# Attention with cached K and V on one core: another order of the first loads and of the first projections

## Chip, cores and metric

One Trainium2 chip, one NeuronCore. The metric is the device time of one execution in microseconds (us), lower is better. The core has TensorE (matmuls; PE in the profile, its weight loads PEld), VectorE (DVE), ScalarE (ACT), GpSimd (POOL) and SyncE (SP); loads are issued by SP and by ScalarE, each on a queue of its own.

## The reference

Two independent problems A and B of the same shape; in each, 16 batches of 80 rows, 32 query heads on 16 K/V heads of 512 cached keys, head size 128:

```
q = (x @ wq) as [batch, 32 heads, 80, 128]          x: [16, 80, 576], wq: [576, 4096], bf16
scores = q @ k^T * 128**-0.5                        k, v: [16, 16, 512, 128], two query heads per K/V head
o = softmax(scores) @ v
out = o as [16, 80, 4096] @ wo                      wo: [4096, 576]
result = concat(A's out, B's out, axis=-1)          [16, 80, 1152]
```

## The kernel before

The work is cut into 128 units: a unit U is one batch and four K/V heads, so 8 query heads of 80 rows. Eight batches (a half) follow each other with the same four K/V heads. Units 0 to 7 are the first half of A's batches, units 8 to 15 the second half, with the same quarter of wq.

For each half and quarter (`goct`) q is projected: operation `qp goct.i.c` (L672) multiplies five chunks of x, transposed, with the 128 columns of head i, for the batches of part c. For the very first one (`goct` 0) part 0 is batches 0 and 1 (160 columns) and part 1 is batches 2 to 7 (480 columns); later ones take four and four (320 columns). VectorE or ScalarE moves the result to `qT` (`qev`, L683 and L684). A's x is loaded by rows (`ldx`, L547) in row blocks of 128, transposed on TensorE (`xtr`, L562) and moved to `xT` (`xev`, L566).

A unit has 640 score rows of 512 keys: five tiles of 128 rows. The first tile gathers the remainders of the four heads (`qkr`, L782: four 32-column matmuls side by side), the others are `qk` (L796). Remainder tiles of two units are done together, except that units 0 and 1 stand alone; so the score groups are unit 0, unit 1, units 2 and 3, units 4 and 5, and so on. Each tile then goes through the maximum on VectorE (`max`, L805), exp with row sums on ScalarE (`exp`, L809), the reciprocal (`rcp`, L815), a scaling on GpSimd (`nrm`, L818), four transposes on TensorE (`tr`, L824) and a copy to `pT` on VectorE (`ptev`, L830 and L832). `pv` (L870) multiplies with V; `oev` (L886) moves the result to `oT`; the output projection is L923. K comes by a transposing load on SP (`ldk`, L746), V by a plain one (`ldv`, L750), the first four V on SP and later ones on ScalarE's queue.

The order on each engine is not written out: a planner (`_Sched`) takes operations with keys, durations and streams and places them greedily, with a model of the two load queues (`_Dma`), and the resulting order is fixed at build time. On the chip each engine runs its list in order and waits on semaphores. Operations of one stream on one engine keep the order of their keys. `XLD` and `WQ1` hold the keys of the first loads of x and wq. Before the first useful matmul TensorE runs `warm` (L507), eight matmuls on ones, and between the transposes of x blocks 1 and 2 `warm2` (L522), four more.

The first loads before, in order, on SP: x of the first half in two pieces (2 and 3 row blocks), x of the second half in two pieces, K of unit 0, the second 1024 columns of wq in four pieces, K of units 1, 2, 3, V of units 0, 1, K of unit 4, V of units 2, 3, K of unit 5. On ScalarE: the first 1024 columns of wq in four pieces.

TensorE's order before: `xtr` of blocks 0 and 1, `warm2`, `xtr` of blocks 2 to 4, then `qp` of heads 0 to 3 for batches 0 and 1, of heads 0 to 3 for batches 2 to 7, of heads 4 to 7 for batches 0 and 1, of head 4 for batches 2 to 7, and then the first score group, with the rest of the projections among the scores.

## Time and profile before

| what | us |
|---|---|
| median of 3 runs | 772.09 (771.92 to 772.26) |
| the profiled execution: its own time | 772.67 |
| the profiled execution: span of its instructions | 770.9 |
| TensorE busy | 762.3 |
| VectorE, ScalarE, GpSimd busy | 680.0, 607.2, 432.3 |

The profile is of one execution; its times start at its first instruction. A row of the timeline gives start, length, engine, line, operation, output and input, shape and count; a row of an engine with a q (SPq, ACTq) is the issuing of a load, not the load itself. The landing of a load is its issue plus the time to landing in the profile's DMA view. Matmuls are pipelined: a single one is listed with some 0.2 to 0.4 us, and in a stream they start every 56 ns (128 columns), 69 (160), 136 (320), 203 (480) or 216 (512).

### The profile page before, as it was taken

Reading aid. Unit: us, or ns where it says so; the run is one execution under the profiler, and the core shown is the slowest. Engines: PE = TensorE matmul, PEld = TensorE weight load, DVE = VectorE, ACT = ScalarE, POOL = GpSimd, SP = SyncE. Lnnn points to the kernel's source line nnn. Section 1 sums busy time; section 2 is a strip of 40 time slices with the busy share of each in tenths; the row PEclk is TensorE's granted clock in tenths of the full one; section 3 lists DMA queues with packets and bytes.
Section 4 is the critical chain, followed back from the end, with each engine's and each line's share of the span. In section 5 each row is a group of like instructions: output and inputs, shape, how many; then the busy total and the mean of one; then the engine's idle time right before and its main releaser. Section 6 shows DMA issues by size and latency. Waiting matters only on the chain.

```text
span 770.9 us, 21081 instructions
## 1 busy us (share of the span) xinstructions
PE 762.3 (99%) x7942; PEld 575.7 (75%) x7942; DVE 680.0 (88%) x1599; ACT 607.2 (79%) x1695; POOL 432.3 (56%) x647
## 2 busy tenths in 40 slices
PE   9899999999999999999999999999999999999998
PEld 5577777777777777777777777777777777777786
DVE  4999999899899999999989989988888988899972
ACT  1888987888888888877778877878888888888860
POOL 1556655655656565655555645654656655565650
PEclk9999999999999999999999999999999999999999
DMA  9999999999999999999999999999999999999931
GB/s 245 235 235 244 217 262 217 228 213 228 206 208 226 248 258 255 239 233 228 205 219 202 220 258 238 249 238 241 220 194 207 198 207 240 241 243 241 248 96 31
DMA packets 422660, 170.76 MB, mean 222 GB/s; under 512 B 319264, under 2 KB 422176, under 8 KB 422560
## 3 DMA queue, kind: packets, MB, share of 16 engines
q1 hardware_dynamic: 355872, 103.22, 74.4%
q10 hardware_dynamic: 66688, 66.20, 29.9%
q8 instruction: 64, 1.05, 0.6%
q14 instruction: 36, 0.29, 0.1%
HBM read 87.46 MB, written 2.95 MB: 117 GB/s over the span
## 4 chain that ended last, share of the span: by engine, by line
PE 94%; DVE 4%; DMA 1%; ACT 1%; issue 0%; SPq 0%
PE ps L672 22%; PE ps L923 20%; PE ps L870 18%; PE ps L824 16%; PE ps L796 13%; PE ps L782 4%; DVE negmax L805 2%; DVE pT L832 1%; DMA acc<-in_A_x_dram 1%; ACT p_sb L809 0%; DVE qT L684 0%; DVE xT L566 0%; DVE pT L830 0%; ACT oT L886 0%; PE ps L562 0%
## 5 line engine op out<-in xcount | busy, mean ns | idle before, releaser
L818 POOL TENSOR_SCALAR p_sb<-p_sb,rinv 128x512 bf16<-128x512 bf16 x640 | 429.9, 692 | 315.6 <-DVE rinv L815 315.4
L809 ACT ACTIVATE p_sb<-ps,negmax 128x512 bf16<-128x512 f32 x640 | 438.8, 691 | 63.8 <-DVE negmax L805 53.9
L805 DVE TENSOR_REDUCE negmax<-ps 128x1 f32<-128x512 f32 x640 | 427.5, 682 | 17.8 <-PE ps L782 9.6
L832 DVE COPY pT<-ps 128x512 bf16<-128x512 bf16 x512 | 210.2, 417 | 15.8 <-PE ps L824 13.3
L870 PE MATMUL ps<-pT,v_sb 128*128 128x160 bf16 x2048 | 219.1, 233 | 0.3 <-issue 0.2
L824 PE MATMUL ps<-ident,p_sb 128*128 128x128 bf16 x2248 | 214.6, 219 | 0.3 <-DVE pT L832 0.2
L672 PE MATMUL ps<-xT,wq_sb 128*128 128x320 bf16 (+2 forms) x1280 | 212.6, 299 | 0.8 <-ACT p_sb L809 0.6
L870 PEld LDWEIGHTS ps<-pT,v_sb 128*128 128x128 bf16 x2048 | 163.3, 98 | 42.5 <-issue 2.0
L796 PE MATMUL ps<-kT,qT 128*128 128x512 bf16 x512 | 193.0, 379 | 1.0 <-ACT p_sb L809 1.0
L824 PEld LDWEIGHTS ps<-ident,p_sb 128*128 128x128 bf16 x2248 | 159.8, 98 | 37.4 <-DVE pT L832 5.9
L923 PE MATMUL ps<-wo_sb,oT 128*128 128x288 bf16 x1280 | 171.3, 286 | 0.1
L672 PEld LDWEIGHTS ps<-xT,wq_sb 128*128 128x128 bf16 x1280 | 116.7, 98 | 54.0 <-ACT oT L886 3.8
L923 PEld LDWEIGHTS ps<-wo_sb,oT 128*128 128x128 bf16 x1280 | 122.7, 98 | 34.2 <-issue 2.1
L886 ACT CAST oT<-ps 128x320 bf16<-128x320 f32 x256 | 108.6, 424 | 44.7 <-PE ps L870 42.0
L809 ACT ACTIVATION_READ_ACCUMULATOR p_sb<-ps,negmax 128x1 f32 x640 | 130.3, 204 | 0.0
L684 DVE TENSOR_SCALAR qT<-ps 128x320 bf16<-128x320 f32 (+2 forms) x138 | 67.4, 488 | 13.4 <-PE ps L672 12.1
L683 ACT ACTIVATE qT<-ps 128x320 bf16<-128x320 f32 (+1 forms) x118 | 51.1, 433 | 31.4 <-PE ps L672 30.9
L796 PEld LDWEIGHTS ps<-kT,qT 128*128 128x128 bf16 x512 | 50.0, 98 | 5.6 <-ACT p_sb L809 2.4
L951 DVE TENSOR_TENSOR osb<-ps,acc 128x288 bf16<-128x288 f32 x40 | 18.3, 457 | 26.9 <-PE ps L923 26.5
L782 PE MATMUL ps<-kT,qT 128*32 128x512 bf16 x512 | 39.6, 384 | 1.9 <-ACT p_sb L809 1.9
L815 DVE RECIPROCAL rinv<-rowsum 128x1 f32<-128x1 f32 (+2 forms) x206 | 34.3, 168 | 6.0 <-ACT p_sb L809 5.7
L830 DVE COPY pT<-ps 128x512 bf16<-128x512 bf16 x50 | 20.8, 416 | 2.3 <-PE ps L824 2.0
(19 smaller groups left out, 47.0 us busy)
## 6 DMA issues: line engine op xcount, KB each, us to landing
v_sb<-in_B_v_cache_dram ACTq DMA_DIRECT2D x64, 512.0 KB, 4.8
v_sb<-in_A_v_cache_dram ACTq DMA_DIRECT2D x60, 512.0 KB, 5.1
wo_sb<-in_A_wo_dram SPq DMA_DIRECT2D x16, 288.0 KB, 5.5
wo_sb<-in_B_wo_dram SPq DMA_DIRECT2D x16, 288.0 KB, 5.0
wq_sb<-in_B_wq_dram SPq DMA_DIRECT2D x16, 256.0 KB, 4.8
out_dram<-osb SPq DMA_DIRECT2D x40, 72.0 KB, 3.3
v_sb<-in_A_v_cache_dram SPq DMA_DIRECT2D x4, 512.0 KB, 5.0
wq_sb<-in_A_wq_dram SPq DMA_DIRECT2D x8, 256.0 KB, 5.1
```

Source lines behind the costliest of these rows:

```text
L672: last = e.matmul(ps[:, vb.phys, 0:n1 - n0], lhsT=wq_sb[:, wsl, ck, i * 128:(i + 1) * 128], rhs=xT[:, half, ck, n0:n1], start=(ck == 0), s ...
L684: return e.tensor_scalar(dst, src, SCALE, None, op0=AluOpType.mult)
L782: last = e.matmul(ps[32 * g4:32 * g4 + 32, vb_.phys, :], lhsT=qT[:, qp_, g4 * 160 + 128:g4 * 160 + 160], rhs=kT[:, ks_, :, g4 * 128:(g4 + ...
L796: return e.matmul(ps[:, vb.phys, :], lhsT=qT[:, qp, gl * 160:gl * 160 + 128], rhs=kT[:, ks, :, gl * 128:(gl + 1) * 128], start=True, stop= ...
L805: return e.tensor_reduce(negmax[:, si:si + 1], ps[:, vb.phys, :], axis=AX.X, op=AluOpType.max, negate=True)
L809: return e.activation(p_sb[:, psl, :], ps[:, vb.phys, :], AF.Exp, bias=negmax[:, si:si + 1], scale=1.0, accum_out=rowsum[:, ss, k:k + 1])
L818: return e.tensor_scalar(p_sb[:, psl, :], p_sb[:, psl, :], rinv[:, ss, k:k + 1], 1.0, op0=AluOpType.mult, op1=AluOpType.mult)
L824: last = e.transpose(psb[:, vt.phys, j * 128:(j + 1) * 128], p_sb[:, psl, j * 128:(j + 1) * 128], ident[:])
L832: return e.tensor_copy(pT[:, pts, :, 0:4, gl * 32:gl * 32 + 32], psb[:, vt.phys, 0:512].rearrange("p (j h c) -> p j h c", j=4, h=4))
L870: last = e.matmul(ps[:, vo.phys, off:off + 160], lhsT=v_sb[:, vs, gl, j * 128:(j + 1) * 128], rhs=pT[:, pts, j, :, gl * 32:gl * 32 + 32], ...
L886: return e.copy(dst, src)
L923: last = e.matmul(ps[:, vb.phys, 0:DC], lhsT=oT[:, hi, rb * 128:(rb + 1) * 128], rhs=wo_sb[:, hi, c3 * DC:(c3 + 1) * DC], start=(hi == 0), ...
```

## The change

The first loads get another order and are cut differently:

- x of the first half comes in three pieces: block 0 on SP, block 1 on ScalarE's queue, blocks 2 to 4 on SP.
- The first 512 columns of wq come in three pieces: chunks 0 and 1 on SP behind the first x piece; chunk 4, and chunks 2 and 3, on ScalarE's queue. The next 512 columns follow on SP.
- Then on SP: K of unit 0, columns 1024 to 1535 of wq, K of unit 1, columns 1536 to 2047, K of units 2 and 3, V of unit 0, x of the second half in two pieces, V of unit 1, K of units 4 and 5, V of units 2 and 3.
- Each of these wq pieces has a semaphore of its own, and so has each of the five pieces of later wq loads per buffer.
- The transposed block 1 of x is moved to `xT` by ScalarE, not VectorE.
- `warm` has seven matmuls; `warm2` and the memset behind it are gone.
- On TensorE `qp` of heads 0 and 1 for batches 0 and 1 comes before the transposes of blocks 2 to 4, then those of heads 2 to 7 for batches 0 and 1, then heads 0 and 1 for batches 2 to 7, then the first score group; the other six for batches 2 to 7 lie among the scores of units 0 and 1.
- The third score group stands ahead of the first probability transpose (`tr0`) instead of behind the first two.
- The planner takes given landing times for these loads (`LAND`) where its model has earlier ones; behind the first 53 operations TensorE's order is the same up to some 500 operations, and then differs by single swaps.

```diff
-NWARM = 8
-NWARM2 = 4
+NWARM = 7
+QP1 = (0.4, 1.1)
...
-XLD = ((-100.0, -60.0), (-25.0, -24.9))
+XLD = ((-100.0, -100.0, -60.0), (-4.0, -3.5))
+LAND = dict(x=((4.0, 4.1, 6.3), (23.3, 24.5)), w=((5.2, 8.0), (12.8, 16.2)), k=(10.3, 14.7, 18.4, 20.4), v=(22.0, 26.0))
...
-WQ1 = -16.8
-WQ1B = 0.02
+WQ1 = ((-90.0, -50.0), (-20.5, -15.5))
...
-                o.done = t_ + DLAT + XM.get(o.stream, 0.0)
+                o.done = max(t_ + DLAT + XM.get(o.stream, 0.0), o.land)
...
-        S.add("pe", -LA - 13.2, em_warm2, reads=[R(("ones",), 0), R(("warm",), 1)], writes=[R(vw2, 0)],
-              name="warm2", stream="X", dur=NWARM2 * 0.3, alloc=[vw2])
...
-        XP = ((0, 2), (2, 5))
+        XP = (((0, 1, "sp"), (1, 2, "act"), (2, 5, "sp")), ((0, 2, "sp"), (2, 5, "sp")))
...
-                    return e.tensor_copy(xT[:, half, :, blk * 128:(blk + 1) * 128],
+                    return (e.copy if (half, blk) == (0, 1) else e.tensor_copy)(xT[:, half, :, blk * 128:(blk + 1) * 128],
...
-                if goct < 2:
-                    parts = ((0, 4, c0, c1), (4, 5, c0, c1))
+                dsem = "d_wq%d" % wsl
+                if goct == 0 and pi == 0:
+                    parts = ((0, 2, c0, c1), (4, 5, c0, c1), (2, 4, c0, c1))
+                elif goct < 2:
+                    parts = ((4, 5, c0, c1), (0, 4, c0, c1))
...
+                    en = "act" if (goct, pi) == (0, 0) and j else "sp"
+                    S.add(en if goct < 2 else WENG, t_ld + 0.01 * j if goct < 2 else 5.0 * cycle[("wq", goct, j)] - 4.0, em_ldw,
...
-                        x = -LA - ((6.0, 3.6), (1.2, 0.5))[i // 4][c] + (0.6 if i < 4 else 0.05 if c == 0 else 1.2) * (i % 4)
+                        x = -LA - (6.0 if c == 0 else QP1[0]) + (0.05 if c == 0 else QP1[1]) * i
...
-                          reads=[R(("wq", wsl, w_, i // 2), wv) for w_ in range(2)] + [R(("wqz",), 0)] + xr,
+                          reads=[R(("wq", wsl, w_, i // 2), wv) for w_ in range(3)] + [R(("wqz",), 0)] + xr,
```

More of the change, by code (lines that the diff above doesn't have):

```diff
@@ L109 @@
                  "alloc", "pri", "after", "xp", "lag", "pre", "start", "done", "mode",
-                 "deps", "signals", "sidx", "waits", "clock", "name", "grid", "hard", "kind")
+                 "deps", "signals", "sidx", "waits", "clock", "name", "land", "grid", "hard", "kind")
 class _Dma:
@@ L516, in bass_concat_heads__gqa_block_cached__gqa_block_cached__near_ridge_kernel @@
         S.add("dve", -980, em_warmend, reads=[R(vw, 0)], writes=[R(("warm",), 1)], name="warmend", stream="warmset")
-        vw2 = S.bank("M")
-        def em_warm2(e, vw=vw2):
-            last = None
-            for _ in range(NWARM2):
-                last = e.matmul(ps[:, vw.phys, :], lhsT=ones, rhs=warm, start=True, stop=True)
-            return last
-        S.add("pe", -LA - 13.2, em_warm2, reads=[R(("ones",), 0), R(("warm",), 1)], writes=[R(vw2, 0)],
-              name="warm2", stream="X", dur=NWARM2 * 0.3, alloc=[vw2])
-        S.add("dve", -LA - 13.1, em_warmend, reads=[R(vw2, 0)], writes=[R(("warm",), 2)], name="warmend",
-              stream="warmset")
         IDENT = R(("ident",), 0)
@@ L543, in bass_concat_heads__gqa_block_cached__gqa_block_cached__near_ridge_kernel @@
             x_ap = probs[0][0]
-            for part, (k0, k1) in enumerate(XP):
+            for part, (k0, k1, en) in enumerate(XP[half]):
                 def em_ldx(e, x_ap=x_ap, half=half, k0=k0, k1=k1):
@@ L548, in em_ldx @@
                                        src.rearrange("(k p) d -> p k d", p=128))
-                S.add("sp", XLD[half][part], em_ldx,
-                      writes=[R(("xs", half * NRT + k_), 0) for k_ in range(k0, k1)], dsem="d_x%d%d" % (half, part),
-                      name="ldx%d.%d" % (half, part), stream="x0", dur=0.5, cost=XC * (k1 - k0))
+                S.add(en, XLD[half][part], em_ldx,
+                      writes=[R(("xs", half * NRT + k_), 0) for k_ in range(k0, k1)], dsem="d_x%d%d" % (half, part), land=LAND["x"][half][part],
+                      name="ldx%d.%d" % (half, part), stream="x0" if half else "xa" if en == "act" else "xs", dur=0.5, cost=XC * (k1 - k0))
             for blk in range(NRT):
@@ L570, in bass_concat_heads__gqa_block_cached__gqa_block_cached__near_ridge_kernel @@
                       stream="X", dur=_mm(5, 128), lat=0.2, alloc=[vb])
-                S.add("dve", x + 0.3, em_xev, reads=[R(vb, 0)], writes=[R(("xT", half, blk), 0)],
-                      name="xev%d" % rb, stream="xev", dur=0.45, lat=0.13)
+                S.add("act" if rb == 1 else "dve", x + 0.3, em_xev, reads=[R(vb, 0)], writes=[R(("xT", half, blk), 0)],
+                      name="xev%d" % rb, stream="xea" if rb == 1 else "xev", dur=0.45, lat=0.13)
         jobs = []
```

32 lines of the change are left out of this document (18 added, 14 removed).

## The prediction

> **What bounds the kernel now.** First the page's busy times and the busy time by stretch (columns: TensorE, its weight loads, VectorE, ScalarE, GpSimd, granted clock, DMA share, GB/s).
>
> ```profile
> PE 762.3 (99%) x7942; PEld 575.7 (75%) x7942; DVE 680.0 (88%) x1599; ACT 607.2 (79%) x1695; POOL 432.3 (56%) x647
> 0.00:26.00 26.00, 23.62 (x161) 13.08 (x161) 16.06 (x34) 8.89 (x23) 4.58 (x11) 1.00 1.02 240
> 26.00:39.00 13.00, 10.22 (x117) 7.20 (x118) 11.88 (x28) 10.30 (x30) 7.93 (x12) 1.00 1.12 237
> 39.00:62.00 23.00, 22.88 (x242) 17.15 (x241) 21.56 (x50) 19.20 (x54) 13.43 (x20) 1.00 1.06 240
> 62.00:120.00 58.00, 57.99 (x636) 43.85 (x635) 55.15 (x129) 50.85 (x146) 37.17 (x57) 1.00 1.07 234
> ```
>
> From 39 us on TensorE is the bound: 22.88 of 23, then 57.99 of 58; from 120 to 720 it idles 0.55 us in all (the same rows, summed). What starts it earlier by some time ends the kernel earlier by that time, and only the first 39 us can give it. Second, the chain that ended last in that stretch (start, length, what):
>
> ```profile
> 8.53 7.83 PE ps L672 x65
> ...
> 26.78 1.29 DVE negmax L805 x2
> 28.17 0.56 DVE negmax L805
> 28.74 0.40 DVE xT L566
> ...
> 37.09 0.61 DVE negmax L805
> 37.73 0.79 ACT p_sb L809 x2
> 38.51 0.41 issue
> 38.92 0.61 PE ps L782 x8
> ```
>
> TensorE's projections hold the start; from the third score group (batches 2 and 3) to the fourth (batches 4 and 5) VectorE does; the "issue" of 0.41 is a K load: issued at 29.92, landing 8.9 us later, at 38.8. Third, the timeline of TensorE and of SP's issues.
>
> ```profile
> 5.74 1.33 PE L522 MATMUL ps<-wo_sb 128*128 128x512 bf16 x4
> 8.37 7.99 PE L672 MATMUL ps<-xT,wq_sb 128*128 128x160 bf16 x65
> 16.29 0.40 PE L782 MATMUL ps<-kT,qT 128*32 128x512 bf16 x4
> 26.12 0.61 PE L782 MATMUL ps<-kT,qT 128*32 128x512 bf16 x8
> 26.89 0.44 PE L562 MATMUL ps<-ident,acc 128*128 128x128 bf16 x5
> 3.31 7.33 SPq L746 DMA_TRANSPOSE kT<-in_A_k_cache_dram  x1
> 13.10 9.57 SPq L746 DMA_TRANSPOSE kT<-in_A_k_cache_dram  x3
> 22.71 1.14 SPq L750 DMA_DIRECT2D v_sb<-in_A_v_cache_dram  x2
> ```
>
> Four marks follow: first projection 8.37, first score 16.29, third group 26.12, fourth group 38.92. Between the first two TensorE only projects, without a gap, though K of batch 0 has been there since 12.8 (3.31 + 9.5 in the DMA view); VectorE has only evictions to do meanwhile.
>
> **To the first projection.** Gone are one of eight matmuls on ones (0.43), the second burst of four with its memset, and their place between the transposes. The x transposes start at 4.72 - 0.43 = 4.29, if x has landed: blocks 0 and 1 (288 KB) landed at 4.6 beside 512 KB of weights; now two loads of 144 KB go first on both queues, about 4.1. Ten transposes at 0.107 (the clock is still half there) end at 5.36. Block 1 is evicted by ScalarE: its rows give 303 ns for 160 columns and 437 for 320, so 134 per 160, some 0.71 for 640, against 0.49 on VectorE; with the 0.25 from transpose to eviction seen at block 1, it ends at 6.3. The ScalarE table load (1.28) moves ahead of it, from 3.45 to about 2.5, under the loads. For the first projection 864 KB must have landed; before, 288 + 512 had by 5.7, and 4.00 to 6.00 moved 387 GB/s: about 5.6, so the eviction is last. First projection 6.35 instead of 8.37. x becomes five loads for four and the weights nine for eight; three issues of 0.5 are ScalarE's instead of four.
>
> **To the first score.** The 15 transposes of blocks 2 to 4 (56 ns: 0.84), 8 x 5 projections of 160 columns (69 ns: 2.77) and 2 x 5 of 480 (203 ns: 2.03) make 5.64, so 12.0. K of batch 0 has 720 KB less ahead (the second half's x), 1.9 us at the 374 GB/s of 7 to 9 us: 10.8, in time. First score 12.0 instead of 16.29.
>
> **To the third group.** In the changed order TensorE has six 480-wide projections (6.08), four 320-wide (5 x 0.136 each, 2.72), eight scores (1.73) and two remainder groups (0.64): 11.2, so 23.2. VectorE needs beside it ten maxima (0.60), five 480-wide (0.575) and three 320-wide evictions (0.40), 10.1 us in the 11.9 from 11.3: it fits, and I add 0.2. Third group 23.4 instead of 26.12, a gain of 2.7, if K of batch 3 is there.
>
> **The loads.** After K0 at 10.8 come half of the second weights, K1, the other half, K2, K3, V0, then x of the second half. Bounds from rows: a copy behind a transpose landed 2.3 us later (first 512 KB of weights, 15.1 after 12.8; 2.5 for 576 KB), a V behind a K 2.6, a K behind a K 2.0 to 2.4. K1 behind copies took 3.0, but a full microsecond of that (18 to 19) moved 5 GB/s, a hole that no load of the kernel made. So K1 15.3 (10.8 + 2.5 + 2.0), weights 17.8, K2 19.9, K3 21.9, V0 24.5, first x piece (288 KB) 25.3. With no gap at any switch it would be 22.1 (1728 KB of copies at 370 GB/s, three K at 2.0, and the 0.7 for x); with 3.0 per switch to K and no further hole, 27.3. I take 25.3. TensorE reaches that transpose 0.77 behind the third group, as before, at 24.2, so it waits 1.1, and the scores behind it wait too. Cover: VectorE has three maxima and one pT eviction from before (2.1 us, from about 24.05) to do, so it starves for 0.3 at most; beyond 25.8 each microsecond costs one.
>
> **To the fourth group.** Order and work are as before: 12.4 (26.12 to 38.51), plus one pT eviction (0.33) now behind the group instead of ahead, plus 0.3 of waiting: 23.4 + 13.0 = 36.4. K of batch 5 is now issued before V of batches 2 and 3, 1 MB less ahead of it than at 38.8, so the 0.41 is gone; those V have until 41 and landed at 33.3 and 34.7. Gain 38.92 - 36.4 = 2.5. If that K were as late as before, 0.
>
> **Behind it.** The queues' order is the same; K loads wait for TensorE and shift with it. Semaphores for each piece of weights take no instruction of an engine. The order on TensorE is the same to about the 27th unit of work and then differs by small swaps: idle time there is 0.55 us over 600, so they can hardly give; what they can lose I bound by 1 us, twice the idle time there is, and take 0.
>
> **Sum.** Span 770.9 - 2.5 = 768.4; the profiled execution took 772.67, 1.77 outside the span, so 770.2; that execution was 0.58 above the median of 772.09. Median after: 769.6. The measurement tells 0.2%, 1.54 us, from no change.
>
> **Rivals.** *TensorE stays at half rate.* Before, its spacing of 512-wide matmuls fell from 427 to 216 ns at 6.4, after 5.1 us without a gap over 0.1; the removed burst is what filled it to there (6.9). Now it idles from 5.36 to 6.35, just there. If the 5.1 us count anew from 6.35, all work to 11.4 is half rate: 2.5 lost; if only the beginning is, 1. Against it: 4.1 unbroken busy microseconds go before. The x wait runs beside and hides part, so the gain is 0.3 to 1.7, say 1.1: 771.0. Chance 0.17. By the Trainium skill (TensorE: Matmul & The Clock Gate, What's actually happening) the full clock comes after a window of about 3.4 us of sustained activity, with windows that run freely; an estimate by it is 1.7 lost at the third group, with the removed burst as the cause. That the change in the trace came 5.1 us after the first matmul agrees with a window not aligned to the kernel.
>
> *The stream is as full as before.* Up to V of batch 1 the same bytes are loaded, and it landed at 28.9. With x at 27.3 the fourth group starts at 27.3 + 11.6 = 38.9 less some of the hole: gain 0.2, 771.9. For it: the K1 row. Chance 0.13.
>
> *Slower: switching costs more.* The K behind two V landed 4.1 us after the second (34.7 to 38.8). If K1 and K2 each cost 4.1 after copies, not 2.0, x comes at 29.4, the transposes block the scores, and the fourth group starts at 41.0: 774.2. It decides from x at 27.3 on (slower by 0.2% from 28.8). Against it: K0, K1 and the K of batch 4 landed 1.5, 3.0 and 1.8 us after the copies ahead of them. Chance 0.11.
>
> The forecast has 0.59; its own range is 768.3 to 770.8, from loads without gaps (0.4 earlier), swaps and a VectorE wait of up to a microsecond. Range for all: 767.4, no load late and a further microsecond of stalls gone, to 772.6, which leaves out the slower rival. Faster by over 0.2%: 0.53 of the forecast, 0.07 of the half rate, 0.05 elsewhere: 0.65. Slower: 0.11 and some of the swaps, 0.12. Same: 0.23.
>
> **What would show it.** First projection near 6.3, first score near 12, third group near 23.4, fourth near 36.4, and no TensorE stretch longer than before after that. Spacing of 133 instead of 69 ns in the first projections shows the half rate; a wait of the transposes into xT of over 1.5 us, with K3 after 24, the late stream. A first score still at 16, or a fourth group not before 38, makes the prediction wrong.

## The result, and the profile after

The changed kernel is slower by 0.40%: its median is 776.04 us (771.10 to 780.27, 22 runs) against 772.38 (771.21 to 775.07, 22 runs) for the kernel before on the same chips, a ratio of 1.0040 with a 95% interval of 1.0023 to 1.0056. The forecast was 769.6. Here and below the medians are of all runs, while the ratios leave out the few that took over 1.5% longer than the quickest of the same kernel. The profiled execution took 777.98, with a span of 776.2, so 1.78 lie outside the span, as before; it is 1.9 us slower than the median, so what it loses is more than the usual loss.

The page's row of TensorE, then the busy time by stretch (columns: stretch, its length, TensorE, weight loads, VectorE, ScalarE, GpSimd, granted clock, DMA share, GB/s):

```profile
PE 762.8 (98%) x7937; PEld 577.8 (74%) x7937; DVE 679.3 (88%) x1596; ACT 610.6 (79%) x1697; POOL 434.1 (56%) x647
...
0.00:26.00 26.00, 21.18 (x137) 12.87 (x138) 13.26 (x28) 8.63 (x20) 4.51 (x11) 0.93 0.90 217
26.00:39.00 13.00, 12.45 (x134) 8.62 (x134) 12.82 (x29) 10.86 (x29) 7.43 (x12) 1.00 1.17 274
39.00:62.00 23.00, 22.88 (x243) 17.21 (x242) 22.45 (x53) 20.12 (x58) 14.03 (x21) 1.00 1.12 244
62.00:120.00 58.00, 58.00 (x636) 43.79 (x635) 55.14 (x129) 50.89 (x147) 37.31 (x57) 1.00 1.06 237
240.00:360.00 120.00, 116.04 (x1216) 87.18 (x1214) 105.97 (x247) 94.42 (x264) 66.82 (x99) 0.99 1.16 229
```

One thing was not as the opening has it: from some 129 us on, 78 of the 640 score tiles have their probabilities transposed by a load on SP's queue (L833, `pT<-p_sb`) and not by TensorE.

The last of these stretches in the kernel before:

```profile
240.00:360.00 120.00, 119.71 (x1268) 90.61 (x1267) 110.09 (x256) 98.26 (x276) 69.88 (x104) 1.00 1.12 242
```

TensorE has as much to do as before (762.8 for 762.3). Two stretches stand out: the first 26 us, where it works 21.18 at a mean clock of 0.93 (before 23.62 at 1.00), and 240 to 360 us, where it idles for 3.96 us (before 0.29). The chain of waits through the beginning, and the timeline of TensorE and of ScalarE's eviction:

```profile
1.82 7.04 DMA wq_sb<-in_A_wq_dram
8.86 0.20 issue
9.05 0.98 PE ps L667 x10
10.04 1.60 PE ps L553 x15
11.64 4.84 PE ps L667 x40
```

```profile
4.20 1.27 PE L553 MATMUL ps<-ident,acc 128*128 128x128 bf16 x10
9.05 0.98 PE L667 MATMUL ps<-xT,wq_sb 128*128 128x160 bf16 x10 [3.58 <-DMA wq_sb<-in_A_wq_dram]
11.43 5.05 PE L667 MATMUL ps<-xT,wq_sb 128*128 128x160 bf16 x40
16.41 0.40 PE L779 MATMUL ps<-kT,qT 128*32 128x512 bf16 x4
27.80 0.61 PE L779 MATMUL ps<-kT,qT 128*32 128x512 bf16 x8
28.80 0.44 PE L553 MATMUL ps<-ident,acc 128*128 128x128 bf16 x5
38.98 0.61 PE L779 MATMUL ps<-kT,qT 128*32 128x512 bf16 x8
5.51 0.69 ACT L557 COPY xT<-ps 128x640 bf16<-128x640 bf16 x1 [1.79 <-PE ps L553]
```

The x transposes are where they were forecast (4.20), and so is ScalarE's eviction of block 1 (5.51 + 0.69 = 6.20). But TensorE then idles for 3.6 us: the first projection waits for the 256 KB of weights issued at 1.82 on ScalarE's queue, which land at 8.86. The clock then falls: granted at half from 9.63 to 13.05, so the 15 transposes of blocks 2 to 4 take 1.60 (from 9.83) instead of 0.84, and the 30 matmuls of 160 columns behind them 2.86 (from 11.43) instead of 2.07 (the row of 40 has ten of 480 columns in it). The first score comes at 16.41 (before 16.29), and the fourth group stands at 38.98, where it stood before (38.92). The gain of 2.5 that was forecast was lost in the first 16 us.

The rest is lost behind 40 us, most of it at one place. TensorE's timeline there, and SP's and ScalarE's load issues:

```profile
305.09 0.61 PE L821 MATMUL ps<-ident,p_sb 128*128 128x128 bf16 x8
309.59 0.44 PE L867 MATMUL ps<-pT,v_sb 128*128 128x160 bf16 x4 [3.89 <-issue]
297.94 2.75 SPq L741 DMA_TRANSPOSE kT<-in_A_k_cache_dram  x1
298.48 0.45 ACTq L745 DMA_DIRECT2D v_sb<-in_A_v_cache_dram  x1
300.80 1.20 SPq L833 DMA_TRANSPOSE pT<-p_sb  x1
```

"Issue" means that the page shows no releaser; the landings do. K issued at 297.94 lands at 307.88 and V issued at 298.48 at 307.51, 9.9 and 9.0 us later (before, at the same place, K and V one after the other: 4.6 and 4.2), and the transposing load of pT in the queue behind them at 309.50. The product with V starts 0.09 later. Behind this hole of 3.89 us come another 3.41 at half clock (from 310.0), which cost 1.7: that is most of what the span behind the fourth group has grown by (737.3 for 732.0). Only one more gap behind 40 us is over half a microsecond: 1.25 at 695.1, ended 0.09 behind a landing K.

### The profile page after: what moved, and what is told of

It is laid out like the page before. It is cut to its first block, busy times and chain, and to the rows that moved or that the text cites. A ratio compares the mean times of both kernels' runs of the same rounds, so it can differ in the third digit from the quotient of the medians.

```text
span 776.2 us, 21051 instructions
## 1 busy us (share of the span) xinstructions
PE 762.8 (98%) x7937; PEld 577.8 (74%) x7937; DVE 679.3 (88%) x1596; ACT 610.6 (79%) x1697; POOL 434.1 (56%) x647
## 2 busy tenths in 40 slices
DMA packets 422692, 170.76 MB, mean 220 GB/s; under 512 B 319296, under 2 KB 422208, under 8 KB 422592
## 4 chain that ended last, share of the span: by engine, by line
PE 94%; DVE 3%; ACT 2%; DMA 1%; issue 1%; ACTq 0%
PE ps L667 22%; PE ps L920 20%; PE ps L867 18%; PE ps L821 16%; PE ps L793 13%; PE ps L779 5%; DVE negmax L802 1%; ACT p_sb L806 1%; DMA wq_sb<-in_A_wq_dram 1%; DVE pT L829 1%; ACT oT L883 0%; DVE xT L557 0%; PE ps L553 0%; DVE qT L679 0%; ACT qT L678 0%
## 5 line engine op out<-in xcount | busy, mean ns | idle before, releaser
L802 DVE TENSOR_REDUCE negmax<-ps 128x1 f32<-128x512 f32 x640 | 426.7, 680 | 25.4 <-PE ps L779 13.2
L667 PEld LDWEIGHTS ps<-xT,wq_sb 128*128 128x128 bf16 x1280 | 118.6, 98 | 55.4 <-issue 6.2
L679 DVE TENSOR_SCALAR qT<-ps 128x320 bf16<-128x320 f32 (+2 forms) x137 | 66.4, 484 | 15.2 <-PE ps L667 14.2
L678 ACT ACTIVATE qT<-ps 128x320 bf16<-128x320 f32 (+2 forms) x119 | 51.9, 436 | 25.2 <-PE ps L667 24.9
```

The costliest lines, as they stand in the source:

```text
L667: last = e.matmul(ps[:, vb.phys, 0:n1 - n0], lhsT=wq_sb[:, wsl, ck, i * 128:(i + 1) * 128], rhs=xT[:, half, ck, n0:n1], start=(ck == 0), s ...
L679: return e.tensor_scalar(dst, src, SCALE, None, op0=AluOpType.mult)
L802: return e.tensor_reduce(negmax[:, si:si + 1], ps[:, vb.phys, :], axis=AX.X, op=AluOpType.max, negate=True)
```

## The experiments

All kernels were timed in five rounds beside the kernel before. Where an "order of before" is kept, the order on every engine, the engine and the PSUM bank of each operation that the planner of the kernel before had put at 100 us of its plan (some 124 of the profile) or later are taken from a table, shifted by one constant; so only what lies ahead differs (in more_loads from some 104 us of the profile on, and in the kernels with loads two cycles later, and those built on them, from some 174). This table has all runs; marks from one profile each, times in us ("behind" is the span less the fourth group; "SP idle" the part of 40 to 100 us in which SP is issuing no load; the expectations give it 1.0 to 1.4 lower):

| kernel | first projection | first score | fourth group | behind | SP idle | median | ratio to before (95%) |
|---|---|---|---|---|---|---|---|
| before | 8.37 | 16.29 | 38.92 | 732.0 | 21.9 | 772.38 | |
| after | 9.05 | 16.41 | 38.98 | 737.3 | 16.4 | 776.04 | 1.0040 (1.0023 to 1.0056) |
| start_only | 8.93 | 15.89 | 38.57 | 739.3 | 6.2 | 777.14 | 1.0043 (1.0017 to 1.0068) |
| body_only | 8.74 | 16.66 | 39.13 | 732.9 | 21.8 | 774.30 | 1.0019 (0.9999 to 1.0038) |
| wq_first_on_act | 7.43 | 12.14 | 37.02 | 735.0 | 3.6 | 772.30 | 0.9997 (0.9974 to 1.0020) |
| start_warm_filler | 8.98 | 14.70 | | | | 776.90 | 1.0044 (1.0017 to 1.0071) |
| x_one_load | 7.91 | 15.26 | 38.07 | 736.0 | 18.5 | 774.45 | 1.0019 (0.9993 to 1.0045) |
| wq_one_queue | 8.11 | 14.45 | 38.54 | 738.7 | 6.2 | 772.59 | 1.0001 (0.9979 to 1.0023) |
| less_v | 9.14 | 17.18 | 39.75 | 734.1 | 14.6 | 774.20 | 1.0020 (0.9998 to 1.0042) |
| more_loads | 9.04 | 16.97 | 39.13 | 731.9 | 15.3 | 774.67 | 1.0038 (1.0009 to 1.0067) |
| wq_first_less_v | 8.09 | 14.43 | 38.52 | 731.6 | 21.9 | 772.09 | 0.9998 (0.9971 to 1.0025) |
| wq_first_wo_later | 8.15 | 15.46 | 39.55 | 731.6 | 22.5 | 772.94 | 1.0000 (0.9968 to 1.0032) |
| wq1_behind_v | 8.19 | 14.54 | 38.49 | 731.8 | 20.6 | 772.29 | 0.9986 (0.9952 to 1.0020) |
| wq1_behind_v_wo_later | 7.96 | 14.31 | 38.26 | 731.8 | 21.9 | 771.83 | 0.9980 (0.9959 to 1.0000) |
| first_loads_first | 7.18 | 13.52 | 37.61 | 731.6 | 10.0 | 772.56 | 0.9980 (0.9957 to 1.0003) |
| first_loads_best | 6.76 | 13.98 | 37.93 | 731.7 | 20.0 | 771.39 | 0.9976 (0.9944 to 1.0008) |
| first_loads_more_warm | 7.08 | 12.32 | 36.28 | 731.7 | 18.4 | 772.63 | 0.9990 (0.9959 to 1.0021) |
| start_wo_later | 8.64 | 15.99 | 39.20 | 731.6 | 15.2 | 774.43 | 1.0008 (0.9979 to 1.0036) |
| best_again | 6.82 | 12.98 | 37.39 | 733.4 | 17.9 | 771.07 | 0.9977 (0.9960 to 0.9995) |
| more_warm_again | 7.03 | 12.14 | 37.24 | 733.7 | 19.5 | 770.88 | 0.9974 (0.9958 to 0.9991) |

The kernels were timed in groups on different chips, and the median of the kernel before went from 772.4 to 774.3 between them; so kernels of different groups are compared by their ratios. The profiled execution of start_warm_filler took 788.58, 11.7 over its median, and its later marks are left out of the table.

Two things limit what the marks can tell. The same start gives other marks in other executions: the first score is at 16.29, 16.66 and 16.97 in the three kernels with the old start (before, body_only, more_loads), and at 16.41, 15.89, 17.18 and 15.99 in four with the changed one (after, start_only, less_v, start_wo_later), so a difference of a microsecond between two profiles says little. And the planner decides the order ahead of the table. In x_one_load, less_v and start_wo_later TensorE's order is start_only's. In wq_one_queue, wq_first_on_act and all kernels built on it, one projection of 480 columns (five matmuls, 1.02 us) stands behind the first score instead of ahead of it, so their first score is 1.0 earlier by the order alone. In more_loads TensorE's order differs from before's from 41.5 us on.

**The start or the later order.** *start_only* has the changed start and the order of before; *body_only* the reverse.

```diff
 # start_only: in arrange(), behind the planner
+for op in ops:
+    if op.name in PLAN_OF_BEFORE and PLAN_OF_BEFORE[op.name].start >= 100:
+        op.start, op.done, op.eng, bank = PLAN_OF_BEFORE[op.name], shifted
```

> The changed start with the old order of everything from the 15th unit or so on: the operations that the planner of before starts at 100 us or later keep that planner's order, engines and banks, shifted by one constant. The traces of before and after agree at the fourth score group (38.92 and 38.98), so the changed start gives nothing as it ran. Theory 'the loss lies in the swaps of the later order': equal to before, 772.4, between 770.5 and 773.5, no TensorE idle time over 2 us after 40 us, one half-rate window near 10 to 13 us. Rival 'the loss comes with the start, by whatever follows when the loads stand otherwise': 775 to 777, like the changed kernel, with idle of some microseconds somewhere behind 40 us.

> The old start with the changed kernel's order from the same place on. Theory 'swaps': slower than before, 774 to 778, with a TensorE wait of over 2 us for a load behind 100 us and the clock at half for 3.4 us behind it. Rival 'with the start': equal to before, 772.4 within 1.

The start alone makes a loss of this size (1.0043); the later order alone some part of it at most (1.0019, an interval that just takes in 1). In body_only's profile the same place is weak as in after's (TensorE idle from 305.62 to 307.35, ended 0.09 us behind a landing pT), for 1.7 us instead of 3.9 and with no half clock behind it. start_only's stall lies elsewhere, at 71.8. By stretch, before and then start_only:

```profile
40.00:70.00 30.00, 29.88 (x323) 22.80 (x321) 28.92 (x69) 26.21 (x73) 17.10 (x26) 1.00 1.08 231
70.00:77.00 7.00, 7.00 (x79) 5.07 (x77) 7.00 (x17) 6.33 (x20) 6.07 (x10) 1.00 1.18 277
77.00:90.00 13.00, 12.99 (x149) 9.90 (x147) 13.00 (x31) 12.23 (x35) 7.06 (x11) 1.00 0.96 217
```

```profile
40.00:70.00 30.00, 29.88 (x323) 22.74 (x321) 29.11 (x69) 26.54 (x75) 17.44 (x26) 1.00 1.14 211
70.00:77.00 7.00, 3.59 (x39) 2.30 (x37) 3.56 (x10) 3.14 (x9) 2.70 (x5) 0.96 1.25 235
77.00:90.00 13.00, 13.00 (x135) 10.12 (x134) 11.70 (x28) 10.57 (x32) 7.89 (x12) 0.89 1.04 218
```

For 30 us TensorE sees nothing (29.88 in both), while the loads move 211 GB/s for 231 with a higher DMA share (1.14 for 1.08). Then it stops. start_only's timeline shows for which load:

```profile
60.55 8.94 SPq L1337 DMA_TRANSPOSE kT<-in_A_k_cache_dram  x1
75.24 0.61 PE L1375 MATMUL ps<-kT,qT 128*32 128x512 bf16 x8 [3.41 <-issue]
```

This K lands at 75.15, 14.6 us after its issue, beside V's landing at 69.41 and 74.91; the scores start 0.09 later. Before, the K issued at 60.10 landed at 67.98. How early K is there tells more than the share: from its landing to its first use, K of the score groups from 50 to 127 us had 2.9 to 9.8 us before, and 3.1, 5.6 and then 0.09 in start_only. after's own K had 3.2 to 7.0 there, no less than before; its stall came 180 us later. Of the 128 K loads none took over 10 us to land before, and six did in start_only.

**Which cut makes the first weights late.** *wq_first_on_act* undoes both cuts of the first loads in start_only; *x_one_load* that of x alone, *wq_one_queue* that of the weights alone.

```diff
 # x_one_load
-XP = (((0, 1, "sp"), (1, 2, "act"), (2, 5, "sp")), ...
+XP = (((0, 2, "sp"), (2, 5, "sp")), ...
 # wq_one_queue
-parts = ((0, 2, c0, c1), (4, 5, c0, c1), (2, 4, c0, c1))
+parts = ((0, 4, c0, c1), (4, 5, c0, c1))
-en = "act" if (goct, pi) == (0, 0) and j else "sp"
+en = "act" if (goct, pi) == (0, 0) else "sp"
 # wq_first_on_act: both
```

> As start_only (old later order), but the first loads are cut as before: x blocks 0 and 1 in one load on SP, the first 512 columns of wq in two (four chunks, then the fifth) at the head of ScalarE's queue. Everything else of the changed start stays. Theory 'the small pieces behind x on ScalarE's queue are what came late (8.9 against 5.7)': first projection at 6.3 to 7.5, no half-rate window at the start or one that ends earlier, fourth group 36 to 37.5, time 769.5 to 771. Rival 'the first megabyte comes late in any cut': first projection at 8.5 or later, time as start_only.

> The changed start with the order of before from some 124 us on (as in start_only), but x of blocks 0 and 1 is one load of 288 KB on SP's queue again; the first 512 columns of the weights stay in three pieces, rows 0 and 1 on SP's queue, the other two on ScalarE's. Theory W (the cut of the weights is what makes them late): the piece of rows 2 and 3 still lands at 8.0 to 8.9, the first projection starts at 8.0 to 9.1, the fourth group at 38 to 39, and the median is 775 to 778 as start_only's 777.1. Theory X (block 1 of x at the head of ScalarE's queue is what pushes them back): the weights land by 7, the first projection starts at 7.4, the fourth group near 37, and the median is 772 to 773 as wq_first_on_act's 772.3.

> As start_only, but the first 512 columns of the weights are two pieces (512 KB and 128 KB) on ScalarE's queue, behind block 1 of x, which stays there. Theory W: they land by 6.5, the first projection starts at 7.3 to 7.9, the fourth group near 37, the median is 772 to 773.5. Theory X: they land at 8 to 9, the first projection starts at 8.3 to 9, and the median is 775 to 778.

The cuts matter together. The last weights that the first projection needs land at 8.44 to 8.94 in the five profiles with both, at 7.71 in x_one_load and 7.86 in wq_one_queue, and at 7.18 to 7.95 in the five with neither (wq_first_on_act, here 7.18, and the four of its kind below). So undoing either cut brings about as much as undoing both, some 1 us. By its marks x_one_load lies between the two theories; wq_one_queue's median (1.0001) went with the weights while its first projection (8.11) did not, and its profiled execution took 778.96, 6.4 over its median, with a stall of 5.9 us at 81.8. wq_first_on_act's marks came as its first theory had them (7.43 and 37.02), its median did not (772.30 for 769.5 to 771): the span behind the fourth group is 735.0, and K issued in 40 to 100 us takes 9.8 us to land (the median; before 7.3). The DMA view by quarters of a microsecond over the first 10 us shows what the cuts do; the kernel before, after, and wq_first_on_act:

```profile
GB/s 0 0 0 0 0 0 0 51 92 143 50 125 288 347 406 380 379 393 377 391 389 387 403 374 324 241 307 316 380 383 384 346 379 379 360 379 383 359 365 314
```

```profile
GB/s 0 0 0 0 0 0 0 83 60 221 300 389 372 317 336 261 111 107 118 149 201 201 235 293 293 350 378 388 355 329 341 352 302 351 316 297 198 138 60 196
```

```profile
GB/s 0 0 0 0 0 0 0 65 198 78 136 273 364 346 372 380 393 380 390 386 392 393 367 281 158 208 220 219 320 328 372 362 337 251 166 68 274 289 291 290
```

Between 4 and 6 us the forecast had 387 GB/s, as before; with the small pieces it is 177 (the mean of eight columns), a hole that begins where the first pieces have landed (3.61 and 3.79). With whole pieces there is no hole there, but one at 6 us, where the 512 KB have landed (5.47; before 5.71) and the second loads of the queues are due.

**The half clock.** *start_warm_filler* is start_only with eight matmuls on ones between the first x transposes and the first projection.

```diff
+S.add("pe", -LA - 13.2, em_warm2, ..., name="warm2")   # eight matmuls of 512 columns on ones
```

> As start_only, with eight matmuls on ones put between the transposes of x blocks 1 and 2, ahead of the first projection, where TensorE waits anyway. Theory 'the wait costs twice, by the 3.9 us and by the half clock behind it': spacing 69 ns from the first projection on, first score about 1.7 earlier than 16.4, fourth group 37.3 to 38.3, time 1 us under start_only. Rival 'half clock hidden by VectorE or loads': the fourth group unchanged near 39, same time as start_only.

The clock stays up (the first score at 14.70 for 15.89, though the first projection is as late), and the time is what it was, 1.0044 for 1.0043. So the half clock costs its time at the start, and giving it back there brought nothing in the end. The fourth group (40.11, behind a stall of 2.02 at 27.3) can't be held against the 37.3 to 38.3 expected, since that execution is so far from the median.

**Fewer, more and later loads.** *less_v* is start_only with half of V of batches 4 to 7 left out (1 MB less, in the loads between 36 and 65 us); *more_loads* the kernel before with 1 MB more there, in loads that nobody reads; *start_wo_later* is start_only with the loads of the output weights two cycles later, nothing left out.

```diff
 # less_v
+n = 2 if 4 <= U < 8 else 4
-src = vc_ap[b:b + 1, 4 * q:4 * q + 4, :, :]...
+src = vc_ap[b:b + 1, 4 * q:4 * q + n, :, :]...
 # more_loads, for units 4 to 7
+S.add("act", 5.0 * U - VK + 0.1, em_scr, writes=[R(("scr",), U)], ..., stream="V")
 # start_wo_later
-r_ = 3.0 + 7.0 * (n // NWC)
+r_ = 5.0 + 5.0 * (n // NWC)
```

> start_only, but of V of batches 4 to 7 only half is loaded (the other half keeps what the buffer held): 1 MB less in the loads issued between 36 and 65 us, all else the same. Theory B (the load queue falls behind the work at the start and is caught up only by stalls): the fourth group stays at 38.6, SP's idle time in 40 to 100 us rises from 5.2 to 12 or more, the gap of 3.6 us at 71.6 and the half clock at 76 are gone, the span behind the fourth group falls from 739 to 733 to 735, and the median from 777.1 to 772 to 773.5. Theory O (the loss lies in the order of the first 100 us itself, or in the half clock at the beginning): 776 to 777.5, with a gap between 60 and 100 us still there.

> The kernel before, with four more loads of 256 KB into a scratch buffer that nobody reads, each behind V of batches 4 to 7 on ScalarE's queue: 1 MB more in the loads issued between 36 and 65 us. From some 104 us on the order is written out as before's. Theory B: 1 MB at 234 GB/s is 4.5 us of the load stream; SP's idle time in 40 to 100 us falls from 20.5 to 16 or less, K loads there take longer than before's 7.3, and if that uses up the reserve the median rises to 775 or more; if the reserve holds it, 773. Theory O: the median stays within 0.7 of before's, no stall.

> start_only (the changed start, 777.1) with the loads of the output weights two cycles of 5.6 us later, nothing left out. Theory B (no reserve in the load stream in 40 to 100 us): SP's idle time in 40 to 100 us rises from 5.2 to 12 or more, the gap of 3.6 us at 71.6 and the half clock behind it are gone, the span behind the fourth group falls from 739.3 to 732 to 734, and the median to 772.5 to 774.5, as less_v's 774.2. Theory O: 776 to 777.5.

The ratios go the way of theory B: the kernel before with 1 MB more is slower by 0.38% (0.09 to 0.67), as much as the change itself; taking or moving loads away brings start_only from 1.0043 to 1.0020 and 1.0008, though these intervals overlap with start_only's, and less_v's median (774.20) is above the 772 to 773.5 expected. more_loads is the weaker of the two halves: its order on TensorE and VectorE is another one from 41.5 us on, so whether its time comes from the loads or from that order is not shown. In less_v and start_wo_later the order is start_only's. The profile of start_wo_later has no gap of 0.3 us from 40 to 720 us and 731.6 behind the fourth group:

```profile
40.00:70.00 30.00, 29.89 (x321) 22.72 (x319) 29.20 (x69) 26.61 (x75) 16.83 (x26) 1.00 1.06 230
70.00:77.00 7.00, 7.00 (x82) 5.14 (x80) 7.00 (x17) 6.33 (x19) 6.07 (x10) 1.00 1.18 278
```

That is the rate of before (230 GB/s at 1.06) in place of 211 at 1.14. more_loads' marks go as theory B has them (K issued in 40 to 100 us takes 8.3 us to land at the median, for 7.3; SP idle 15.3), and its median, 774.67, is between the 773 and the 775 that it named; but its profiled run had no stall either, so the place of its loss can't be shown. Stalls fall in some runs and not in others, and SP's idle time, which theory B named as a mark, is a poor one: x_one_load has 18.5 us of it and still a stall of 3.0 at 49.9, first_loads_first 10.0 and none.

**The start put right, with the stream eased.** *wq_first_less_v* and *wq_first_wo_later* ease the loads behind wq_first_on_act in the same two ways. *wq1_behind_v* moves the last 512 columns of the second weights behind V of batch 1, and the first x piece of the second half ahead of V of batch 0; *wq1_behind_v_wo_later* has both.

```diff
 # wq1_behind_v, on wq_first_on_act
-WQ1 = ((-90.0, -50.0), (-20.5, -15.5))
+WQ1 = ((-90.0, -50.0), (-20.5, -1.5))
-XLD = ((-100.0, -60.0), (-4.0, -3.5))
+XLD = ((-100.0, -60.0), (-8.5, -3.5))
 # LAND follows, and with it some 27 places of TensorE's order
```

> wq_first_on_act (the start that gains 1.9 us up to the fourth group and gives 3.0 back behind it), but of V of batches 4 to 7 only half is loaded (the other half keeps what the buffer held): 1 MB less in the loads issued between 36 and 65 us. Theory B (what is gained at the start is given back because the load stream has no reserve in 40 to 100 us): SP's idle time there rises from 2.5 us to 10 or more, the fourth group stays near 37.0, the span behind it falls from 735.0 to 732.5 to 733.5, and the median from 772.3 to 769.5 to 771. Theory O (it is given back by the order of the work, whatever the loads do): the median stays at 772 to 773.

> wq_first_on_act with nothing left out: the four loads of 288 KB of the output weights, one each 5.6 us from about 44 us on, start two such cycles later, and the loads of weights behind them move by two cycles at most, until a free cycle at about 140 us takes up the shift; the order from some 174 us on is before's. 576 KB less have been asked for at any time between 55 and 140 us. Theory B: SP's idle time in 40 to 100 us rises from 2.5 us to 6 or more, the fourth group stays near 37.0, the span behind it is 732.5 to 734, the median 769.5 to 771.5. Theory O: 772 to 773.

> wq_first_on_act, but the last 512 columns of the second set of weights (640 KB on SP's queue) go behind V of batch 1 instead of ahead of K of batch 2, and the first x piece of the second half ahead of V of batch 0. Theory B: K of batches 2 and 3 land some 2 us earlier (20 and 22), x of the second half by 24.5 instead of 27.9, so TensorE does not wait for it, the third group starts near 24.5 and the fourth at 35.5 to 36.5; the stream has as much to load by 40 us as before, so SP has no more idle time in 40 to 100 us than 2.5, and part is given back behind: the median is 770.5 to 772.5. A rival (what starts earlier ends earlier, the stream has reserve): 769.5 to 770.5.

> wq1_behind_v with the loads of the output weights two cycles later, as in wq_first_wo_later; nothing left out. Theory B: fourth group at 35.5 to 36.5 and 733 to 734.5 behind it, the median 769 to 771, the fastest of these kernels. Theory O: as wq1_behind_v.

Behind the fourth group all four are where theory B puts them, or better: 731.6 to 731.8, without a stall. For wq1_behind_v that is a miss of theory B, which gave it no more idle time of SP than wq_first_on_act has (3.6; it has 20.6) and expected part of the gain to be lost again. Of the 128 K loads 8 took over 10 us to land in wq_first_on_act, and 1, 0, 1 and 0 in these four. Their starts are not where they were expected: the fourth group comes at 38.3 to 39.6, not at 37.0 or 35.5 to 36.5, and so the medians of three missed what theory B expected (772.09, 772.94 and 771.83), while wq1_behind_v's 772.29 lies in its range. With the start as it was in wq_first_on_act, easing the loads shows in the profiles and not in the medians (0.9998 and 1.0000 for 0.9997). In all four TensorE idles 2.1 to 2.5 us ahead of the first projection, until the 64 KB of weights (fifth chunk; the expectations call them 128) have landed (7.7 to 8.0), and most of the projections that follow run at half clock. The start of wq_first_on_act's profile (12.14, 37.02) was a lucky one: wq_first_less_v and wq_first_wo_later have the same first loads and the same order, and their first score is at 14.43 and 15.46. In wq1_behind_v x of the second half came early as meant (23.16 for 27.87), and it gained nothing: the fourth group is at 38.49 for 38.52 in wq_first_less_v.

*first_loads_first* puts, on wq_first_on_act, these 64 KB second on SP's queue and x of blocks 2 to 4 behind the weights on ScalarE's; *first_loads_best* does so on wq1_behind_v_wo_later; *first_loads_more_warm* adds two matmuls on ones.

```diff
-XP = (((0, 2, "sp"), (2, 5, "sp")), ...
+XP = (((0, 2, "sp"), (2, 5, "act")), ...
-en = "act" if (goct, pi) == (0, 0) else "sp"
+en = "act" if (goct, pi, j) == (0, 0, 0) else "sp"
 # first_loads_more_warm
-NWARM = 7
+NWARM = 9
```

> As wq_first_on_act (order of before from some 124 us on), but the 128 KB of weights go on SP's queue directly behind x of blocks 0 and 1, and x of blocks 2 to 4 (432 KB) on ScalarE's queue behind the 512 KB of weights. Theory E (bandwidth shared with loads that are not needed yet delays the last part): the 128 KB land at 5.7 to 6.4, the first projection starts at 6.2 to 6.8, the first score at 11.8 to 12.5, the fourth group at 36.5 to 37 (x of the second half still at 27.5 or later holds it). Theory S (the second load of a queue lands 2 us behind the first whatever it is): 128 KB at 7.2 to 8, first projection at 7.4 to 8.2, as before. The median, since the loads behind 26 us are as in wq_first_on_act: 771 to 773 by both.

> wq1_behind_v_wo_later (nothing left out; 771.8, its profile without a stall behind 40 us, 731.8 behind the fourth group) with the first loads as in first_loads_first. Theory E: first projection 6.2 to 6.8, first score 11.8 to 12.5, fourth group 35.5 to 36.5, median 769 to 770.5, faster than before by 0.25% or more. Theory S: first projection 7.4 to 8.2, median 771 to 772.

> first_loads_best with nine matmuls on ones at the start for seven, so that TensorE is busy to about 4.6 instead of 3.8 and idles less before the x transposes and the first projection. If the half clock at the beginning (3.4 us of it cost 1.7 us of work) is what is left: no half clock between 6 and 14 us, the first score up to 1.7 us earlier than in first_loads_best where that has one, median lower by 0.5 to 1.5. If not: within 0.4 of first_loads_best, or 0.2 to 0.9 slower where x lands ahead of the end of the nine.

> first_loads_best once more, on another chip perhaps. Theory (start and load stream were all that was lost): as its profile, 1.2 below before's span, and more where the half clock stays away: median 770 to 771.5 where before is at 772.4, ratio 0.997 to 0.999. Rival (rare stalls eat it): ratio 0.999 to 1.001.

> first_loads_more_warm once more. Theory: as its profile, 2.9 below before's span: median 769 to 770.5 where before is at 772.4, ratio 0.996 to 0.998, and 0.5 to 1.5 below best_again. Rival (rare stalls eat it, or the clock's windows fall otherwise): ratio 0.999 to 1.001, within 0.4 of best_again.

The 64 KB now land at 6.40 to 6.94 in the five profiles, between the two theories (E 5.7 to 6.4, S 7.2 to 8): some of the delay was bandwidth shared with loads not needed yet, and some stays with the second load of a queue: they land 0.4 to 1.2 us behind the 512 KB at the head of the other one. first_loads_best's median, 771.39, is in the range of theory S, not of E (769 to 770.5), and first_loads_more_warm's, 772.63, is above all that was expected. The profile puts the wait for the first projection down to ScalarE's eviction in the four with the stream eased; by their ends that is so in best_again (eviction 6.77, weights 6.40), as the prediction had it for the changed kernel, while in the other three the weights are as late or up to 0.26 later. TensorE and ScalarE in more_warm_again:

```profile
1.24 4.02 PE L1106 MATMUL ps<-wo_sb 128*128 128x512 bf16 x9 [1.24 <-DVE wo_sb L1099]
5.06 0.78 PE L1149 MATMUL ps<-ident,acc 128*128 128x128 bf16 x10
7.03 0.85 PE L1263 MATMUL ps<-xT,wq_sb 128*128 128x160 bf16 x10 [1.19 <-ACT xT L1153]
8.96 3.25 PE L1263 MATMUL ps<-xT,wq_sb 128*128 128x160 bf16 x35
12.14 0.40 PE L1375 MATMUL ps<-kT,qT 128*32 128x512 bf16 x4
5.88 0.69 ACT L1153 COPY xT<-ps 128x640 bf16<-128x640 bf16 x1 [2.70 <-PE ps L1149]
```

Here the 9 matmuls on ones last until the transposes at 5.06, the idle time ahead of the first projection is 1.19, and the 30 matmuls of 160 columns run at full clock (2.08 from 8.96 on, where after took 2.86; the row of 35 has five of 480 columns in it). The first score is at 12.14. Both versions beat the kernel before: 0.9977 (0.9960 to 0.9995) and 0.9974 (0.9958 to 0.9991), though on the chip where they were timed first, on which before itself spread from 771 to 782, the intervals took in 1. Against the changed kernel it is 0.7% (0.9974 over 1.0040, from different chips). The two more warm matmuls give no more than the interval hides (771.07 and 770.88; 0.5 to 1.5 was expected). Both of the last profiles still have a stall, of 1.74 and 2.02 us at 48, ended 0.09 and 0.10 us behind a landing K. Their fourth groups, too, start 0.09 behind a landing K (37.30 and 37.15), as before's did.

## Why the prediction was wrong, point by point

**To the first projection: the step that failed.** The step said 864 KB land "about 5.6, so the eviction is last". They landed at 8.86, and the first projection came 2.70 us late (9.05). The rate was taken from a kernel with two whole pieces at the head of each queue, and carried over to one with five small ones, of which the 256 KB stood third on its queue. The runs divide the 3.3 us. Some 1 us goes with the cutting into small pieces on both queues (8.4 to 8.9 with both cuts, 7.2 to 7.95 with neither). Some 1 us goes with loads that ran beside it: with the same bytes first in line on both queues they land at 6.4 to 6.9 (first_loads_first and its followers). The other 0.8 to 1.3 stays even there. The profile before had a row that says so: its 64 KB of the fifth chunk, second on ScalarE's queue, landed at 7.30, 1.6 behind the 512 KB, and the step counted only what had landed by 5.7. What is "first in the order of need" on one queue is not so on the chip: 432 KB of x and 576 KB of later weights on SP's queue ran beside it. The Trainium skill (DMA: Bandwidth & Descriptors, Queues, rings and completion order) has each DMA engine take turns between the queues that have work, by packets. The DMA view before agrees: from 8 to 9 us the two queues moved 195 and 179 KB. I had not asked what the other queue moves meanwhile.

**To the first score.** 5.64 was forecast between these marks, 7.36 measured: 1.72 more, which is half of the 3.41 us at half clock. So the rival of the half rate came in, with a wait of 3.6 us for weights as its cause where it had named one of 1. The estimate by the Trainium skill that stands there (TensorE: Matmul & The Clock Gate, What's actually happening) was 1.7 lost, and the trace agrees with its size. The cause given with it was the removed burst; with eight matmuls on ones in that wait the clock did stay up (start_warm_filler).

**To the third group.** 11.4 forecast (with the 0.2 added), 11.39 measured. K was in time for all of it.

**The loads.** x of the second half landed at 27.75, not 25.3: K0 0.97 late (11.77), K1 0.58 more, the second weights 0.55, K2 0.68, the rest to two tenths as forecast. That is 0.45 above my upper bound of 27.3, but the transposes did not wait for it at all, since everything ahead was late too: x was there before the third group began (27.80), and they follow at 28.80 without a gap on TensorE, behind four transposes of probabilities that now stand ahead of them. The slower rival's condition, x at 27.3 or later, was met and its mechanism was not at work; wq1_behind_v, with x at 23.16, was no quicker to the fourth group than wq_first_less_v. (The 1728 KB in the lower bound should be 1664; the 22.1 comes out with those.)

**To the fourth group.** 13.0 forecast, 11.18 measured, 1.8 better. I had carried over 12.4 from before as VectorE's work; after has one maximum, and one eviction of pT, fewer between these marks, and TensorE was busy for 10.63 of 11.18 instead of 10.03 of 12.80. That K of batch 5 would no longer hold the group was right: it landed at 35.55, 3.4 us ahead. Together: 36.4 + 2.70 + 1.72 - 0.01 - 1.82 = 38.99, the mark to a hundredth.

**Behind it: the second step that failed.** I took 0 and bounded the loss at 1 us by TensorE's idle time before (0.55 us in 600). It was 5.3 in the profiled execution; the medians differ by 3.7. An idle time near nothing says that nothing was late in that run, not how much later it might be. The DMA share that I had read with it (1.06 and 1.07 from 39 to 120 us) doesn't say it either: it counts packets that overlap, and reads 2.62 from 17 to 18 us. The distance from a landing to its first use does, and for K it was 2.9 to 9.8 us before, so a load has to come several microseconds later than usual to cost anything. Such loads came: 9.9 and 12.9 us for K around after's stall, 14.6 at start_only's, 15.1 at wq_one_queue's, where before has 9.9 at the most. What is shown is that, of the stalls of over 1.2 us from 40 to 700 us, in all profiles, each ends within 0.1 us of a landing transposing load (K or pT); that start_only's ratio is above 1; and that five profiles with fewer or later loads, or with the weights moved, have no stall. That easing the loads takes the loss out of the time is likely (1.0020 and 1.0008 for 1.0043) but not shown, since the intervals overlap, and more_loads has another order besides its loads. Why the loads are slower beside the changed start (211 GB/s at a share of 1.14 for 231 at 1.08) was not settled; that K's transposing and V's copying, issued closer together, slow each other down is the reading that fits the landings (9.9 and 9.0 us for 4.6 and 4.2), and no run has changed that alone. body_only leaves open whether the later swaps add to it (1.0019, 0.9999 to 1.0038); after's stall lies where body_only has one too.

**What held.** That the start can gain: with other first loads and the later loads moved, the time came to 0.9974 of before, against the 0.9968 forecast for the changed kernel. That these are so near is in part luck, since the marks are not the forecast's. In the five profiles of first_loads_first and its followers the first projection is at 6.76 to 7.18 (6.35 forecast), the third group at 25.37 to 27.11 (23.4), the fourth at 36.28 to 37.93 (36.4). Their first score, 12.14 at the earliest, has one projection of 480 columns behind it that the forecast's 12.0 has ahead; in the changed kernel's order it would be some 13.2, an estimate from 12.14 and the 1.02 of that projection.

## What to carry to other kernels

For an order of need over two queues, ask for each load what the other queue moves at that time, and put what is not needed yet behind the needed on both, in whole pieces: here that brought the first projection from 9.05 to 6.8 to 7.2. Before moving work forward, look at how much earlier the loads behind it can come: a change of the first loads can be paid for by a stall tens of microseconds later (71.8 us in start_only). Take a mark from several profiles before reading a microsecond from it. And a bound on what a part can lose is not to be taken from the idle time of the run at hand, but from the distance of each load to its first use.

## What the hardware showed that was not expected

Half clock does not take a wholly idle window. In the 3.41 us up to the fall TensorE was idle for 1.75 in first_loads_best (two gaps, 1.06 and 0.69) and for 2.06 in wq1_behind_v, and the next 3.41 were at half clock; gaps of 0.91, 1.19 and 1.50 ahead of the first projection (first_loads_more_warm, more_warm_again, start_warm_filler) left it up. If windows of 3.41 us are counted on from the recorded changes of the clock, one with 1.85 us idle (before, from 37.07) and one with 1.94 (wq_one_queue, from 80.36) left it up too, so the idle time alone does not decide it. The Trainium skill (TensorE: Matmul & The Clock Gate, What's actually happening) has half clock after at least one idle window of about 3.4 us; the length agrees with the trace, the idleness does not: 1.35 to 1.66 us of work in the window did not prevent it. Nor does the clock come up at a set time: with the same seven matmuls on ones it was full from 3.90 us in first_loads_first and only from 9.66, 13.61 and 14.01 in best_again, wq_first_wo_later and less_v, so part of the spread between the starts is chance.

A transposing load of K, which took 5.7 us from issue to landing at the median before and 9.9 at the most, took up to 14.6 in start_only and 15.1 in wq_one_queue, with V's copies landing beside it. And the kernel before with 1 MB of loads that nobody reads, 0.6% of the 170.76 MB that it moves, took 0.38% longer with TensorE the bound throughout; how much of that is its other order is open.
